# Sums of an expert's weights made by accumulating transfers, and seven products for every pair of token blocks

## The chip, the cores and the metric

The kernel runs on one core of one Trainium2 chip. The core has TensorE (matrix products into PSUM), VectorE, ScalarE and GpSimd (elementwise work), the queues that issue transfers (here those of SP and of GpSimd), and 16 DMA engines that move the data. In the profile's rows these engines are PE (with PEld for loading a matmul's stationary operand), DVE, ACT, POOL and SP. The metric is the device time of one execution in microseconds (us), lower is better. Three runs of the kernel before took 690.27, 690.28 and 691.59 us.

## The reference

Two parts follow each other. The first is attention over sorted blocks: a matrix per head is balanced by five rounds of normalisation, mixes the blocks of keys and values, and ordinary softmax attention follows. The second is a mixture of experts over the 3072 tokens that come out, and the change lies in it:

```
P = exp(logits - max); eight rounds of normalising rows and columns   # gates, tokens x 8
for e in range(8):
    h  = np.maximum(x @ w1[e], 0.0)      # x: 3072 x 512, w1[e]: 512 x 1024
    ye = h @ w2[e]                       # w2[e]: 1024 x 512
    out += P[:, e:e + 1] * ye
```

All experts process all tokens. The inputs are float32 in HBM; the products run on bfloat16 operands.

## The kernel before

Attention comes first, woven with expert 0, which is computed with plain products. Experts 1 to 7 run in the main loop. An expert's tokens are cut into three blocks of 1024 (p = 0, 1, 2), so the loop has 21 passes over (e, p); I call a pass a **pair**, numbered 0 to 20. Pair n computes the hidden layer of its own (e, p) and, at the same time, the output of the pair before it. Each pair has four steps i, which I call **slots**.

*First product, `hidden` (L475).* x and W1 are each seen as 2 x 2 blocks, and the product is made by seven block products where eight would be needed, in the manner of Strassen and Winograd: sums of W1's blocks (s1, s2, s4 in the tile `wc`, s3 over W1's own block a21) are multiplied by sums of x's blocks (`xc`, made by `sum_x` on VectorE), and the partial products are added in PSUM and on the way out. A slot makes 14 matmuls of 512 columns. VectorE's TENSOR_ADD_SAT adds two partial products and clamps below at zero in one instruction (this is the ReLU); ScalarE copies partial products p1, u2, p5 and applies the last ReLU. The four results of a slot are called c11, c12, c21, c22 and land in the tile `hT`.

*Second product.* `output` (L536) makes it with eight products: 16 matmuls of 512 columns in a slot, and two gathers (`gather`, L527: VectorE adds the gated PSUM result to the output tile `osbl`). `output7` (L561) makes it with seven: 28 matmuls of 256 columns and six gathers. It needs sums of h's blocks (`hs`, made by `sum_h` at L553: four GpSimd instructions of 128x512 a slot) and of W2's blocks (t1 to t4 in the tile `w2s` or `w2e`, made by `sum_w2`). Slots 1 to 3 use `output7` from pair 2 on; slot 0 uses `output`, since the sums of h for slot 0 would need the last result of the slot just ended. Pair 1, and the last pair's output after the loop, use `output` throughout.

*Weights' sums.* `sum_w` (L322) and `sum_w2` (L415) are generators of eight GpSimd additions or subtractions of 128x512 each. They wait in a list, and `sums` draws one of them per slot, or three at a pair's end (and in pair 1). For expert 1, `sum_w` runs during the last batch's attention. `load_w1` and `load_w2` (L82, L87) load an expert's weights from HBM and cast them to bfloat16; they are issued from GpSimd's queue. All of these are pinned, so that GpSimd takes them in the order of the program.

*Order.* The order of each engine's instructions is fixed when the kernel is built: the matmuls of `hidden` and of the output are generators that `take` (L605) draws from in turn, a few matmuls each; what is pinned keeps the program's order; the rest is placed by a scheduler. Each engine then runs its own list strictly in order and waits where an operand is not ready. Tiles come from pools with a fixed number of buffers: three for `hs`, two for `hT`, W1 and W2, so a load of expert e+1 waits for the last reader of expert e-1. Before the main loop, `balance` (L437) normalises the gates in a chain of small VectorE instructions and matmuls (L466), woven with the end of expert 0 and the hidden layer of pair 0.

Of the kernel before, what the change touches and what calls it, by code (L numbers as in the profile page):

```python
# [13 lines left out]
F32 = mybir.dt.float32  # L14
BF16 = mybir.dt.bfloat16
AF = mybir.ActivationFunctionType
# [9 lines left out]
def kernel(  # L26
# [11 lines left out]
    nc = tc.nc  # L38
# [43 lines left out]
    def load_w1(e):  # L82
        w1t[e] = wp.tile([128, 4, F], BF16, name="w1e")
        pin(nc.gpsimd.dma_start(out=w1t[e],
                                in_=moe_w1[e].rearrange("(kk k) f -> k kk f", k=128)))
# [231 lines left out]

    wct = {}  # L320

    def sum_w(e):  # L322
        wct[e] = (wcq if e % 2 == 0 else wcp).tile([128, 3, 2, F // 2], BF16, name="wc")
        for kk in range(2):
            a11, a21 = (w1t[e][:, kk, f:f + 512] for f in (0, 512))
            a12, a22 = (w1t[e][:, 2 + kk, f:f + 512] for f in (0, 512))
            s1, s2, s4 = (wct[e][:, j, kk, :] for j in range(3))
            for a, b, o, c in ((a21, a22, ALU.add, s1), (s1, a11, ALU.subtract, s2),
                               (a11, a21, ALU.subtract, a21), (a12, s2, ALU.subtract, s4)):
                pin(nc.gpsimd.tensor_tensor(out=c, in0=a, in1=b, op=o))  # L330
                yield

    with tc.tile_pool(name="ps0", bufs=8, space=bass.MemoryType.PSUM,
                      reuse_waits="tile") as ps0:
# [32 lines left out]
    with ExitStack() as c2:  # L367
        pa = c2.enter_context(tc.tile_pool(name="pa", bufs=8, space=bass.MemoryType.PSUM,
                                           reuse_waits="tile"))
        bank1 = lambda shape, dt: pa.tile(shape, dt, name="bank", tag="bank")  # L370
        ebank = lambda: bank1([128, 512], F32)
        for bb in range(1, B):
            ex = expert0(bb - 1, lambda: mps.tile([128, 8, 384], BF16, name="hTs"),
                         ebank, ebank, pin)
            at1, left = attention(bb, bank1), 16 if bb == 1 else 26
            for _ in range(28 - left):
                next(ex)
            last = 3 if bb + 1 < B else 0
            left -= last
            cut = lambda k: left * k // 12  # L380
            weave(at1, ex, 5, cut(5))
            if bb + 1 < B:
                load_batch(bb + 1, [(x, 0, 8) for x in "vkq"])
                build_r(bb + 1, nc.gpsimd, 4)
            else:
                load_w1(1)
# [23 lines left out]
    def bank():  # L410
        return bk.tile([128, 512], F32, name="bk")

    w2s = {}

    def sum_w2(e):  # L415
        w2s[e] = (wcp.tile([128, 4, 4, Dm // 2], BF16, name="w2e") if e % 2 else
                  w2q.tile([128, 4, 4, Dm // 2], BF16, name="w2s"))
        for k in (0, 2):
            b11, b12 = (w2t[e][:, k:k + 2, d:d + 256] for d in (0, 256))
            b21, b22 = (w2t[e][:, 4 + k:6 + k, d:d + 256] for d in (0, 256))  # L420
            t1, t2, t3, t4 = (w2s[e][:, j, k:k + 2, :] for j in range(4))
            for a, b, c in ((b12, b11, t1), (b22, t1, t2), (b22, b12, t3), (b21, t2, t4)):
                pin(nc.gpsimd.tensor_tensor(out=c, in0=a, in1=b, op=ALU.subtract))
                yield

# [3 lines left out]
    def sum_x(p):  # L429
        ta, tb = (slice(1024 * p + 512 * i, 1024 * p + 512 * i + 512) for i in range(2))  # L430
        b11, b12, b21, b22 = (xtT[:, k:k + 2, t] for k in (0, 2) for t in (ta, tb))
        x1, x2, x4 = (xc[:, j, :, 512 * p:512 * p + 512] for j in range(3))
        for a, b, c in ((b12, b11, x1), (b22, x1, x2), (b22, b12, b12), (b21, x2, x4)):
            pin(nc.vector.tensor_tensor(out=c, in0=a, in1=b, op=ALU.subtract))
            yield

    def balance():  # L437
# [37 lines left out]
    def hidden(e, p, i, hT):  # L475
        ta, tb = (slice(1024 * p + 512 * j, 1024 * p + 512 * j + 512) for j in range(2))
        fs = slice(128 * i, 128 * i + 128)
        xs = slice(512 * p, 512 * p + 512)

        def add(ps, wa, xa, first):  # L480
            for kk in range(2):
                nc.tensor.matmul(ps, wa[:, kk, :], xa[:, kk, :],  # L482
                                 start=(first and kk == 0), stop=(kk == 1),
                                 skip_group_check=True)
# [24 lines left out]
        u2 = wide("u2")  # L509
        nc.scalar.copy(u2, u)  # L510
        yield
        v = bank()
        add(v, s1, x1, True)
        p5 = wide("p5")
        nc.scalar.copy(p5, v)  # L515
        yield
        add(u, s3, x3, False)
        nc.vector._custom_dve(TENSOR_ADD_SAT, out=c22, in0=u, in1=p5, s0=TOP, s1=0.0)  # L518
        yield
        add(v, s4, b22, False)  # L520
        nc.vector._custom_dve(TENSOR_ADD_SAT, out=c12, in0=v, in1=u2, s0=TOP, s1=0.0)  # L521
        yield
        add(u, a22, x4, False)
        nc.scalar.activation(out=c21, in_=u, func=AF.Relu)  # L524
        yield

    def gather(e, t, c, ps):  # L527
        o = osbl[:, t, c:c + ps.shape[-1]]
        nc.vector.scalar_tensor_tensor(out=o, in0=ps, scalar=glog[:, t, e:e + 1], in1=o,  # L529
                                       op0=ALU.mult, op1=ALU.add)  # L530

    def store(e, t):
# [15 lines left out]
            yield  # L548


    hs = {}

    def sum_h(i, hT):  # L553
        s = hs[i] = hsp.tile([128, 4, 4, 128], BF16, name="hs")
        a11, a21, a12, a22 = (hT[:, f:f + 4, t + 128 * i:t + 128 * i + 128]
                              for f in (0, 4) for t in (0, 512))
        for a, b, o, c in ((a21, a22, ALU.add, 0), (s[:, 0], a11, ALU.subtract, 1),
                           (a11, a21, ALU.subtract, 2), (a12, s[:, 1], ALU.subtract, 3)):
            nc.gpsimd.tensor_tensor(out=s[:, c], in0=a, in1=b, op=o)  # L559

    def output7(e, p, i, hT):  # L561
        a, b = 8 * p + i, 8 * p + 4 + i
# [17 lines left out]
        add(x0, hT[:, 4:8, ha], b21, True)  # L580
        yield
        add(u, s2, t2, False)
        gather(e, a, 256, u)
        yield
        add(x1, s1, t1, False)
        gather(e, b, 256, x1)
        yield
        add(u, s3, t3, False)
        gather(e, b, 256, u)
        yield  # L590
        add(x1, s4, b22, False)
        gather(e, a, 0, x)
# [34 lines left out]
    take([chain, xs])  # L627
    xs = sum_x(2)
    last = (1, 0, hT)
    queue = [sum_w2(1)]  # L630

    def sums(n):
        while n and queue:
            if next(queue[0], 0) is None:
                n -= 1
            else:
                queue.pop(0)

    for n in range(1, 3 * (E - 1)):
        e, p = 1 + n // 3, n % 3  # L640
        if n == 1 or p == 0 and e + 1 < E:
            load_w1(e + 1)
            queue.append(sum_w(e + 1))
        hT = htp.tile([128, 8, 1024], BF16, name="hT")
        for i in range(4):
            if last[0] == 1:
                scale0([8 * last[1] + i, 8 * last[1] + 4 + i])
            if n > 1 and i < 3:
                sum_h(i + 1, last[2])
            next(xs, 0)  # L650
            sums(3 if n == 1 or i == 3 else 1)
            take([hidden(e, p, i, hT),
                  (output7 if n > 1 and i else output)(*last[0:2], i, last[2])])
        if n == 1 or p == 0 and e + 1 < E:
            load_w2(e + 1)
            queue.append(sum_w2(e + 1))
        last = (e, p, hT)
    for i in range(4):
        take([output(*last[0:2], i, last[2])])
# [30 lines left out]
```

## Time and profile before

| | before |
|---|---|
| median of 3 runs | 690.28 us |
| the profiled execution's own time | 690.48 us |
| its span | 688.7 us |
| TensorE busy | 666.7 us (97%) |
| VectorE busy | 474.5 us (69%) |
| GpSimd busy | 432.4 us (63%) |
| ScalarE busy | 298.0 us (43%) |
| DMA queue of GpSimd, share of 16 engines' span | 25.5% |
| DMA queue of SP | 3.4% |
| first matmul of pair 0 / pair 1 / pair 2 | 145.2 / 174.8 / 200.6 us |
| first matmul of pair 20, end of the last matmul | 645.4 / 684.1 us |

The profile is of one execution, and its span leaves out what lies around the first and last instruction; hence the two times. Busy time is an average over very different stages: attention and the start (to 145 us), the balancing chain (to 175), and the main loop, in which every pair lasts the same 24.7 us. A question about the main loop is answered by one pair. In a row of a group stand the line, the engine, the operation, what is written and read with shapes, the number of instructions, then busy time and the mean of one in ns, then the idle time of the engine just before them and what ended it. DMA-issuing instructions have rows, but are not counted as busy.

### The profile page before, as it was taken

To read this page: it belongs to the slowest core of one execution; us is meant where nothing else is said; L and a number is where in the kernel's file an instruction comes from. 1 tells how busy PE (TensorE), PEld (TensorE's weight loads), DVE (VectorE), ACT (ScalarE), POOL (GpSimd) and SP (SyncE) were. 2 spreads that over 40 slices of the span, in tenths; PEclk is the share of its full clock that TensorE was granted. 3 is DMA by queue.
4 is the path that set the end of the run, shared out by engine and by line. 5 is a ranking of instruction groups with operands and counts; after the bars stand their busy time and mean duration, and the time that the engine had idled before them with its cause. 6 is when DMAs were issued, how large, how long until landed. Compare 5 with 4: busy or idle time off the path is not lost.

```text
span 688.7 us, 12265 instructions
## 1 busy us (share of the span) xinstructions
PE 666.7 (97%) x4784; PEld 404.4 (59%) x4784; DVE 474.5 (69%) x968; ACT 298.0 (43%) x550; POOL 432.4 (63%) x411
## 2 busy tenths in 40 slices
PE   2999999999999999999999999999999999999997
PEld 1757666644446556556656655655665665565563
DVE  6627555578757778667767776767776777676773
ACT  3747646345953333343333433333333433334330
POOL 4532324202737987978977987789795998637520
PEclk9899999999999999999999999999999999999999
DMA  9897833403210340030302140034003120001213
GB/s 146 164 218 120 140 77 63 62 1 62 30 32 1 62 61 1 1 63 9 54 0 35 28 62 1 1 62 61 1 1 62 25 38 0 1 1 63 91 65 151
DMA packets 31755, 36.51 MB, mean 53 GB/s; under 512 B 2000, under 2 KB 24016, under 8 KB 31696
## 3 DMA queue, kind: packets, MB, share of 16 engines
q0 software_dynamic: 26400, 27.82, 25.5%
q1 hardware_dynamic: 5296, 7.90, 3.4%
q8 instruction: 37, 0.61, 0.4%
q14 instruction: 22, 0.18, 0.1%
HBM read 52.45 MB, written 6.29 MB: 85 GB/s over the span
## 4 chain that ended last, share of the span: by engine, by line
PE 91%; DVE 5%; ACT 1%; DMA 1%; issue 1%; SPq 0%; DVEq 0%
PE bk L482 36%; PE oacc L573 25%; PE oacc L542 13%; PE bank L297 5%; PE bank L304 5%; PE bank L232 2%; PE bank L152 1%; PE bank L243 1%; PE bank L215 1%; PE bank L196 1%; DMA vsb<-vs 1%; DVE cs L464 0%; PE bk L297 0%; PE bk L466 0%; PE bank L183 0%
## 5 line engine op out<-in xcount | busy, mean ns | idle before, releaser
L529 DVE SCALAR_TENSOR_TENSOR osbl<-oacc,glog,osbl 128x256 f32<-128x256 f32 (+1 forms) x396 | 214.8, 554 | 122.4 <-PE oacc L542 61.3
L559 POOL TENSOR_TENSOR hs<-hT 128x512 bf16<-128x512 bf16 x114 | 130.0, 1154 | 63.0 <-DVE hT L521 62.8
L482 PE MATMUL bk<-xtT,w1e 128*128 128x512 bf16 x504 | 149.9, 379 | 0.2 <-ACT u L510 0.2
L573 PEld LDWEIGHTS <-hs 128*128 128x128 bf16 x912 | 89.2, 98 | 59.0
L542 PE MATMUL oacc<-w2e,hT 128*128 128x512 bf16 x432 | 119.8, 379 | 0.0
L524 ACT ACTIVATE hT<-bk 128x512 bf16<-128x512 f32 x84 | 50.1, 597 | 153.0 <-PE bk L482 152.9
L482 PE MATMUL bk<-xc,wc 128*128 128x512 bf16 x336 | 99.9, 379 | 0.0
L573 PEld LDWEIGHTS <-hT 128*128 128x128 bf16 x684 | 66.9, 98 | 44.2
L510 ACT COPY u<-bk 128x512 f32<-128x512 f32 x84 | 49.2, 586 | 92.9 <-PE bk L482 92.8
L573 PE MATMUL oacc<-w2e,hs 128*128 128x256 bf16 x588 | 88.2, 273 | 0.0
L573 PE MATMUL oacc<-w2e,hT 128*128 128x256 bf16 x576 | 86.4, 273 | 0.0
L482 PEld LDWEIGHTS <-w1e 128*128 128x128 bf16 x672 | 65.8, 98 | 30.5 <-issue 1.4
L542 PEld LDWEIGHTS <-hT 128*128 128x128 bf16 x432 | 42.3, 98 | 50.8
L506 DVE CUSTOM_DVE_ANT_0 hT<-bk,p 128x512 bf16<-128x512 f32 x84 | 58.0, 691 | 18.4 <-PE bk L482 14.8
L559 POOL TENSOR_TENSOR hs<-hT,hs 128x512 bf16<-128x512 bf16 x57 | 65.8, 1154 | 1.5
L559 POOL TENSOR_TENSOR hs<-hs,hT 128x512 bf16<-128x512 bf16 x57 | 65.7, 1152 | 0.0
L502 ACT COPY p<-bk 128x512 f32<-128x512 f32 x84 | 49.2, 586 | 31.3 <-PE bk L482 31.3
L482 PEld LDWEIGHTS <-wc 128*128 128x128 bf16 x504 | 49.3, 98 | 22.2
L518 DVE CUSTOM_DVE_ANT_0 hT<-bk,p 128x512 bf16<-128x512 f32 x84 | 57.8, 688 | 4.5 <-PE bk L482 1.4
L515 ACT COPY p<-bk 128x512 f32<-128x512 f32 x84 | 49.3, 586 | 25.4 <-PE bk L482 25.4
L521 DVE CUSTOM_DVE_ANT_0 hT<-bk,u 128x512 bf16<-128x512 f32 x84 | 57.3, 682 | 0.1
L482 PE MATMUL bk<-xc,w1e 128*128 128x512 bf16 x168 | 50.0, 379 | 0.0
(106 smaller groups left out, 777.6 us busy)
## 6 DMA issues: line engine op xcount, KB each, us to landing
w1e<-in_moe_w_dram POOLq DMA_DIRECT2D x8, 1024.0 KB, 8.2
w2e<-in_moe_w_dram POOLq DMA_DIRECT2D x8, 1024.0 KB, 8.9
out_dram<-osbl SPq DMA_DIRECT2D x24, 256.0 KB, 2.0
vt<-in_v_dram POOLq DMA_DIRECT2D x3, 768.0 KB, 10.6
vsb<-vs SPq DMA_DIRECT2D x16, 97.5 KB, 4.6
vsb<-vs POOLq DMA_DIRECT2D x16, 97.5 KB, 4.1
qt<-in_q_dram POOLq DMA_DIRECT2D x4, 384.0 KB, 12.8
kt<-in_k_dram POOLq DMA_DIRECT2D x4, 384.0 KB, 13.4
```

The source lines that it names most:

```text
L482: nc.tensor.matmul(ps, wa[:, kk, :], xa[:, kk, :], start=(first and kk == 0), stop=(kk == 1), skip_group_check=True)
L502: nc.scalar.copy(p1, u)
L506: nc.vector._custom_dve(TENSOR_ADD_SAT, out=c11, in0=w, in1=p1, s0=TOP, s1=0.0)
L510: nc.scalar.copy(u2, u)
L515: nc.scalar.copy(p5, v)
L518: nc.vector._custom_dve(TENSOR_ADD_SAT, out=c22, in0=u, in1=p5, s0=TOP, s1=0.0)
L521: nc.vector._custom_dve(TENSOR_ADD_SAT, out=c12, in0=v, in1=u2, s0=TOP, s1=0.0)
L524: nc.scalar.activation(out=c21, in_=u, func=AF.Relu)
L529: nc.vector.scalar_tensor_tensor(out=o, in0=ps, scalar=glog[:, t, e:e + 1], in1=o, op0=ALU.mult, op1=ALU.add)
L542: nc.tensor.matmul(oacc, hT[:, fb, tt * 128:(tt + 1) * 128], w2t[e][:, fb, :], start=(fb == 0), stop=(fb == 7))
L559: nc.gpsimd.tensor_tensor(out=s[:, c], in0=a, in1=b, op=o)
L573: nc.tensor.matmul(ps, h[:, fb, :], w[:, fb, :], start=(first and fb == 0), stop=(fb == 3), skip_group_check=True)
```

## The change

1. The sums of W1's and W2's blocks are no longer made by GpSimd's arithmetic. SP copies one block into the place of the sum (SBUF to SBUF), and GpSimd issues a transfer that reads another block from HBM in float32 and adds it to what is there (`more`, `accum_op=ALU.add`). s2 starts as a copy of s1, s4 as a copy of s2, and likewise t2 of t1 and t4 of t2, so an expert has two chains of alternating copies and accumulating transfers: three copies and four transfers for W1, four copies and four transfers for W2.
2. [...] So the signs of some sums are turned: s2, t1 and others hold the negative of what they held. The sums of x are turned to match (two of four `sum_x` instructions become scalar_tensor_tensor, with a factor of -1). Where a product comes out negative, the clamp keeps the negative side (c22) and ScalarE negates it afterwards, the last ReLU takes scale=-1, and two of `output7`'s gathers use the negated gates `gneg`.
3. `output7` is used in slot 0 as well, from pair 2 to pair 20. The sums of h for slot 0 are made in two parts: three of the four blocks in slot 3 of the pair before, the last one at the start of slot 0.
4. The steps of the weights' sums and the loads have fixed slots (`plan`, `jobs`): every second slot for one expert's chain (every slot for W2 of expert 1), and within a slot behind the sums of h.

```diff
+    def more(out, src, kk, c):
+        rows, cols = out.shape[1:]
+        pin(nc.gpsimd.dma_start(
+            out=out, in_=src.rearrange("(kk k) f -> k kk f", k=128)[:, kk:kk + rows, c:c + cols],
+            accum_op=ALU.add))
 
     def sum_w(e):
+        load_w1(e)
         wct[e] = (wcq if e % 2 == 0 else wcp).tile([128, 3, 2, F // 2], BF16, name="wc")
-        for kk in range(2):
...
-                pin(nc.gpsimd.tensor_tensor(out=c, in0=a, in1=b, op=o))
-                yield
+        s1, s2, s4 = (wct[e][:, j] for j in range(3))
+        a21 = w1t[e][:, 0:2, 512:1024]
+        nc.sync.dma_start(out=s1, in_=a21)
+        yield
+        more(s1, moe_w1[e], 2, 512)
+        more(a21, moe_w1[e], 0, 0)
+        nc.sync.dma_start(out=s2, in_=s1)
+        yield
+        more(s2, moe_w1[e], 0, 0)
+        nc.sync.dma_start(out=s4, in_=s2)
+        yield
+        more(s4, moe_w1[e], 2, 0)
+        yield
+
+    def sum_w2(e):
+        if e > 1:
+            load_w2(e)
...
+        t1, t2, t3, t4 = (w2s[e][:, j] for j in range(4))
+        for t in (t1, t3):
+            nc.sync.dma_start(out=t, in_=w2t[e][:, 0:4, 256:512])
+        yield
+        more(t1, moe_w2[e], 0, 0)
+        more(t3, moe_w2[e], 4, 256)
+        nc.sync.dma_start(out=t2, in_=t1)
+        yield
+        more(t2, moe_w2[e], 4, 256)
+        nc.sync.dma_start(out=t4, in_=t2)
+        yield
+        more(t4, moe_w2[e], 4, 0)
+        yield
...
-        for a, b, c in ((b12, b11, x1), (b22, x1, x2), (b22, b12, b12), (b21, x2, x4)):
-            pin(nc.vector.tensor_tensor(out=c, in0=a, in1=b, op=ALU.subtract))
+        for a, b, c, turned in ((b11, b12, x1, False), (x1, b22, x2, True),
+                                (b22, b12, b12, False), (x2, b21, x4, True)):
+            pin(nc.vector.scalar_tensor_tensor(out=c, in0=a, scalar=-1.0, in1=b, op0=ALU.mult,
+                                               op1=ALU.subtract) if turned else
+                nc.vector.tensor_tensor(out=c, in0=a, in1=b, op=ALU.subtract))
...
-        nc.vector._custom_dve(TENSOR_ADD_SAT, out=c22, in0=u, in1=p5, s0=TOP, s1=0.0)
+        nc.vector._custom_dve(TENSOR_ADD_SAT, out=c22, in0=u, in1=p5, s0=0.0, s1=-TOP)
+        nc.scalar.activation(out=c22, in_=c22, func=AF.Copy, scale=-1.0)
...
-        nc.scalar.activation(out=c21, in_=u, func=AF.Relu)
+        nc.scalar.activation(out=c21, in_=u, func=AF.Relu, scale=-1.0)
...
-    def sum_h(i, hT):
-        s = hs[i] = hsp.tile([128, 4, 4, 128], BF16, name="hs")
...
+    def sum_h(i, hT, f0=0, f1=4):
+        if f0 == 0:
+            hs[i] = hsp.tile([128, 4, 4, 128], BF16, name="hs")
+        s1, s2, s3, s4 = (hs[i][:, j, f0:f1] for j in range(4))
...
+    nc.scalar.activation(out=gneg, in_=glog, func=AF.Copy, scale=-1.0)
+    jobs = {}
+    def plan(work, at, every):
+        for n in range(4):
+            jobs.setdefault(at + every * n, []).append(work)
+    plan(sum_w2(1), 4, 1)
     for n in range(1, 3 * (E - 1)):
         e, p = 1 + n // 3, n % 3
         if n == 1 or p == 0 and e + 1 < E:
-            load_w1(e + 1)
-            queue.append(sum_w(e + 1))
+            plan(sum_w(e + 1), 4 * n, 2)
+            plan(sum_w2(e + 1), 4 * n + 4, 2)
         hT = htp.tile([128, 8, 1024], BF16, name="hT")
         for i in range(4):
             if last[0] == 1:
                 scale0([8 * last[1] + i, 8 * last[1] + 4 + i])
+            if n > 1 and i == 0:
+                sum_h(0, last[2], 3)
             if n > 1 and i < 3:
                 sum_h(i + 1, last[2])
+            if i == 3 and n + 1 < 3 * (E - 1):
+                sum_h(0, hT, 0, 3)
             next(xs, 0)
-            sums(3 if n == 1 or i == 3 else 1)
+            for work in jobs.get(4 * n + i, ()):
+                next(work)
             take([hidden(e, p, i, hT),
-                  (output7 if n > 1 and i else output)(*last[0:2], i, last[2])])
-        if n == 1 or p == 0 and e + 1 < E:
-            load_w2(e + 1)
-            queue.append(sum_w2(e + 1))
+                  (output7 if n > 1 else output)(*last[0:2], i, last[2])])
```

More of the change, by code (lines that the diff above doesn't have):

```diff
@@ L316, in expert0 @@
             yield from expert(0, bb * S + c * 384, 384, hsb, hbank, obank, keep, hold)
-    wct = {}
+    wct, w2s = {}, {}
+    def more(out, src, kk, c):
[3 more added lines that the diff above has]
+            accum_op=ALU.add))
     def sum_w(e):
+        load_w1(e)
         wct[e] = (wcq if e % 2 == 0 else wcp).tile([128, 3, 2, F // 2], BF16, name="wc")
-        for kk in range(2):
[L325 to L329, printed above, removed]
-                pin(nc.gpsimd.tensor_tensor(out=c, in0=a, in1=b, op=o))
-                yield
+        s1, s2, s4 = (wct[e][:, j] for j in range(3))
[14 more added lines that the diff above has]
+            load_w2(e)
+        w2s[e] = (wcp.tile([128, 4, 4, Dm // 2], BF16, name="w2e") if e % 2 else
+                  w2q.tile([128, 4, 4, Dm // 2], BF16, name="w2s"))
+        t1, t2, t3, t4 = (w2s[e][:, j] for j in range(4))
[11 more added lines that the diff above has]
+        yield
     with tc.tile_pool(name="ps0", bufs=8, space=bass.MemoryType.PSUM,
@@ L385 @@
             else:
-                load_w1(1)
                 sums = sum_w(1)
@@ L411, in bank @@
         return bk.tile([128, 512], F32, name="bk")
[L413 to L424, printed above, removed]
     xc = xcp.tile([128, 3, 2, N // 2], BF16)
@@ L523, in hidden, with gather @@
         add(u, a22, x4, False)
-        nc.scalar.activation(out=c21, in_=u, func=AF.Relu)
+        nc.scalar.activation(out=c21, in_=u, func=AF.Relu, scale=-1.0)
         yield
-    def gather(e, t, c, ps):
+    def gather(e, t, c, ps, sign=1):
         o = osbl[:, t, c:c + ps.shape[-1]]
-        nc.vector.scalar_tensor_tensor(out=o, in0=ps, scalar=glog[:, t, e:e + 1], in1=o,
+        g = glog if sign > 0 else gneg
+        nc.vector.scalar_tensor_tensor(out=o, in0=ps, scalar=g[:, t, e:e + 1], in1=o,
                                        op0=ALU.mult, op1=ALU.add)
@@ L548, in output @@
             yield
+    gneg = mpc.tile([128, NT, E], F32)
     hs = {}
-    def sum_h(i, hT):
-        s = hs[i] = hsp.tile([128, 4, 4, 128], BF16, name="hs")
-        a11, a21, a12, a22 = (hT[:, f:f + 4, t + 128 * i:t + 128 * i + 128]
+    def sum_h(i, hT, f0=0, f1=4):
+        if f0 == 0:
+            hs[i] = hsp.tile([128, 4, 4, 128], BF16, name="hs")
+        s1, s2, s3, s4 = (hs[i][:, j, f0:f1] for j in range(4))
+        a11, a21, a12, a22 = (hT[:, f + f0:f + f1, t + 128 * i:t + 128 * i + 128]
                               for f in (0, 4) for t in (0, 512))
-        for a, b, o, c in ((a21, a22, ALU.add, 0), (s[:, 0], a11, ALU.subtract, 1),
-                           (a11, a21, ALU.subtract, 2), (a12, s[:, 1], ALU.subtract, 3)):
-            nc.gpsimd.tensor_tensor(out=s[:, c], in0=a, in1=b, op=o)
+        for a, b, o, c in ((a21, a22, ALU.subtract, s1), (s1, a11, ALU.subtract, s2),
+                           (a11, a21, ALU.subtract, s3), (a12, s2, ALU.add, s4)):
+            nc.gpsimd.tensor_tensor(out=c, in0=a, in1=b, op=o)
     def output7(e, p, i, hT):
@@ L582, in output7 @@
         add(u, s2, t2, False)
-        gather(e, a, 256, u)
+        gather(e, a, 256, u, -1)
         yield
@@ L588, in output7 @@
         add(u, s3, t3, False)
-        gather(e, b, 256, u)
+        gather(e, b, 256, u, -1)
         yield
@@ L629 @@
     last = (1, 0, hT)
[L630 to L637, printed above, removed]
+    nc.scalar.activation(out=gneg, in_=glog, func=AF.Copy, scale=-1.0)
[4 more added lines that the diff above has]
+    plan(sum_w2(1), 4, 1)
     for n in range(1, 3 * (E - 1)):
```

## The prediction

> **What bounds the kernel now.** I read the busy shares first, then the stretches of one pair of token blocks, the list of waits, GpSimd's groups and timeline, and the landing times of transfers. From the page:
>
> ```profile
> PE 666.7 (97%) x4784; PEld 404.4 (59%) x4784; DVE 474.5 (69%) x968; ACT 298.0 (43%) x550; POOL 432.4 (63%) x411
> ```
>
> TensorE is the bound. The stretches of one pair, cut at the first matmul of each slot (a slot is one step i of the inner loop); columns: window, its length, then busy time (instructions) of each engine, granted clock, DMA share, GB/s:
>
> ```profile
> 398.27:404.75 6.48, 6.48 (x32) 2.94 (x30) 3.54 (x6) 2.72 (x5) 6.46 (x7) 1.00 0.92 126
> 404.75:410.83 6.08, 6.08 (x44) 4.09 (x42) 4.76 (x9) 2.00 (x4) 6.08 (x6) 1.00 0.25 42
> 410.83:416.91 6.08, 6.08 (x45) 4.12 (x43) 4.87 (x10) 2.36 (x5) 6.00 (x7) 1.00 0.00 0
> 416.91:422.99 6.08, 6.08 (x45) 4.12 (x43) 4.87 (x10) 2.36 (x5) 2.28 (x3) 1.00 0.00 0
> ```
>
> A slot with eight products in the second layer (the first row) lasts 6.48 us, one with seven 6.08, and TensorE fills both. The same pattern runs from pair 2 to pair 20. The waits from 200 to 665 us name no TensorE line; GpSimd's are:
>
> ```profile
> POOL hs L559 <- DVE hT L521: 62.8, 9, 15.0
> POOL w1e L84 <- PE bk L482: 25.5, 5, 6.9
> POOL w2e L89 <- PE oacc L573: 11.3, 5, 3.1
> ```
>
> GpSimd has slack, but it runs in order, and TensorE reads its sums. Its groups, and the transfers:
>
> ```profile
> L559 POOL TENSOR_TENSOR hs<-hT 128x512 bf16<-128x512 bf16 x114 | 130.0, 1154 | 63.0 <-DVE hT L521 62.8
> L89 POOL DMA_DIRECT2D w2e<-in_moe_w_dram x8 | 7.4, 928 | 11.3 <-PE oacc L573 11.3
> L84 POOL DMA_DIRECT2D w1e<-in_moe_w_dram x8 | 6.4, 794 | 62.6 <-PE bk L297 36.7 <-PE bk L482 25.5 <-issue 0.3
> ```
> ```profile
> w1e<-in_moe_w_dram POOLq DMA_DIRECT2D x8, 1024.0 KB, 8.2
> w2e<-in_moe_w_dram POOLq DMA_DIRECT2D x8, 1024.0 KB, 8.9
> out_dram<-osbl SPq DMA_DIRECT2D x24, 256.0 KB, 2.0
> ```
> And where GpSimd meets a pair's end (slot start at 422.99):
> ```profile
> 416.75 2.40 POOL L423 TENSOR_TENSOR w2e<-w2e 128x512 bf16<-128x512 bf16 x2
> 422.87 2.27 POOL L559 TENSOR_TENSOR hs<-hT 128x512 bf16<-128x512 bf16 x2 [3.73 <-DVE hT L521]
> ```
>
> Two such instructions in a row end 2.27 apart and not 2.31: one costs 1.115 us of GpSimd's time. T below is the start of a pair's slot 0.
>
> **Seven products in slot 0.** From pair 2 to pair 20, 19 slots change from 16 matmuls of 512 columns to 28 of 256: 19 x (6.475 - 6.08) = -7.5 us. VectorE's gathers go from 2 x 0.745 to 5 x 0.480 + 0.745 in that slot, which makes it one of the 4.87 us slots above; three of these in a row already run at 6.08. TensorE's order in the loop is the old pattern, repeated. This is the gain; the rest is whether something makes TensorE wait.
>
> **Signs.** (1) ScalarE negates c22, 84 x 0.59 (the row of its 128x512 copies): 50 us on an engine with 2.36 of 6.08 us used. In the slot it sits between the copy to p5 and the last Relu. VectorE ends c22 4.9 us into a slot, so the negation ends near 5.5, ahead of c12 at 5.95, which the sums need anyway: 0. If ScalarE were full, up to 0.59 a slot. (2) Two of the four sums per token block become scalar_tensor_tensor of 128x1024. The tensor_tensor beside no GpSimd work took 0.68; by the slope between the gathers (0.480 at 256 columns, 0.745 at 512) the new form takes up to 1.27, so 0 to +0.6 each. Two lie in the balancing chain after 145 us, where TensorE idled 2.25 us over 140 to 175 waiting for column sums. TensorE's new order puts about 0.4 us more matmuls into some of those intervals. I take +0.3, ends -0.5 and +1.2. (3) The negated gates: one 0.45 us activation after that chain, first used in pair 2. (4) Other constants: 0.
>
> **Weights' sums leave GpSimd.** 16 instructions an expert go, 7 x 16 x 1.115 = 125 us, off the path: GpSimd waits 63 us for hT. In return come, per expert, eight accumulating transfers that GpSimd issues and seven copies that SP issues; each of GpSimd's waits for a copy, each copy for a transfer before it. SP has nothing else to do before the stores of the last expert. Issue: 0.54 (96 packets) to 0.93 (1024 packets) by the rows; I take 0.65 for W1's (256) and 0.8 for W2's (512).
>
> A 1 KB packet of a plain casting load, which reads 2 KB of float32, holds its DMA engine 0.098 us (packets of the trace, as the others here); one of 1040 bytes copied out of SBUF 0.047 undisturbed, 0.133 under other traffic. No accumulating transfer is in this trace. A packet of one reads both its source and its destination: 0.098 + 0.047 = 0.145 as estimate, so 16 packets on each engine take 2.35 us. The lower end is the plain load's 1.6 us; the upper is 4.7, three times that, as the 1040-byte packets rose to three times theirs when they met other reads. I take 2.35, since packets in this trace follow the bytes that they read.
>
> **Hidden sums for slot 0.** Eight more GpSimd instructions per pair: four of 384 columns in slot 3, four of 128 in the next slot 0. By 1.115 for 512 and about 0.2 fixed (its 128x128 rows take 0.2 to 0.3): 0.85 and 0.36, so 4.85 per pair, 92 us in all. The budget per pair of 24.3 us: 1.4 + 12 x 1.115 + 3.4 = 18.2 us, and transfers' issue, at most five, 3.8. It fits if GpSimd does not stand still.
>
> **Where it stands still.** In six pairs (2, 4, 7, 10, 13, 16) GpSimd's order is: rest of sum 0 and sum 1, transfer s2, load W2, sums 2 and 3, transfer s4, transfers t1 and t3, then sum 0 of the next pair. Sum 0 starts at T-0.1 (above), so s2 is issued at T+5.8 and the load of W2 at T+6.5. Its packets stand behind s2's: those begin 0.7 after the issue's end, T+7.15, and end at 9.5; W2's take 7.05 (125.61 to 132.66 for the load issued at 123.97), so 16.55, plus 0.65 for the copy of s2 to s4 in between and 0.2 to land: T+17.4. SP then copies t1 and t3, 0.6 apart, 32 packets of 512 bytes per engine each. A 256 KB store lands in 2.0 with 0.66 us of packets (8 of 2 KB at 0.083); with 0.87 (0.027 each, on the line through the 1040-byte and 2 KB packets), and s4's transfer beside them, I get T+20.5 and T+21.6. GpSimd was free for t1 at T+17.0, so it stands 3.5 us; t3 is issued by T+22.4. Then sum 0 for the next pair, 3.4 + 1.1 until its s2 is complete: T+26.9. TensorE needs it in the third group of the next slot 0: groups of the two layers alternate, 0.434 us each, so that group starts 2.17 into the slot and takes its last operand at 2.5, T+26.8. Stall 0.2 us x 6 = +1.2. If transfers cost as plain loads: T+21.5, no stall, 0.7 spare; at three times, T+24.8, 2.5 x 6 = +15.
>
> In other pairs the margin is wider. Where W1 is loaded: issue T+5.8, landing +8.2, copy +2.4 = T+16.5, when GpSimd has just finished sum 3 at T+15.6. The old code blocked GpSimd on the release of W1 and W2 (25.5 and 11.3 us of waits); both loads now stand behind sum 1, when their buffers are long free.
>
> **The start.** For expert 1, load W1 is still issued at 106.7 and lands at 114.9. Then three times a copy (2.4) and a transfer (1.5 to start, 2.35, 0.2): 134 for s4's landing; the old sums ended near 124. Its first use is some 7 us after 145.2, so 0; at 10 us a transfer it would begin to cost. GpSimd's other work of that stretch (queries' copies) precedes it; W2's load behind it moves from 124 to about 132, and is needed after 174. For W2 of expert 1 the last transfer, t4, now stands behind slot 3's sum 0, issue near 198, landing 202 to 203; needed at 206: 0, with 3 us to spare.
>
> **Sum.** 690.48 (profiled execution: span 688.7 and 1.8 around it; it is 0.2 over the median) - 7.5 + 1.2 + 0.3 = 684.5.
>
> **Rivals.** (a) Slower: accumulating transfers, or their issue, are dearer than that. Place: the six pair ends above. The sum turns where each stall passes 1.2 us, t3 issued past T+23.4: packets of 0.21 us (2.1 times plain), or 0.3 us more for each issue. At three times 690.5 - 7.5 + 15 + 0.3 = 698, at four times 708. For it: s2's transfer stands in W2's ring, and nothing here shows its rate. Against: packets follow bytes read. (b) No stall at all, 683.3, if they cost as plain loads. (c) The second read costs a whole packet like the first: 2 x 0.098, 3.1 us, t3 issued at T+23.2, a stall of 1.0, 689.3. For it: no packet here reads two places, so the sum of two rows is untried; against: the destination's bytes are half the source's.
>
> [...]
>
> (d) VectorE holds slot 0 at 6.48, as four dense slots now follow each other: 690.5, no change. Against: 4 x 4.87 is 19.5 of 24.3. (e) The balancing chain or the start waits 2 to 4 us more: 686 to 688; for it, that chain alone made TensorE wait before.
>
> **How the numbers follow.** The runs spread 1.3 us, 0.2%, about what can be told from no change (688.9 to 691.7). The forecast with (b): 0.40, 682.5 to 685.5. Larger stalls under 1 us, or (e), up to 688.9: 0.15. Within 0.2%, (c) and (d): 0.09. Slower, by (a): 0.36; of this some 0.15 lies over 706, and below 681.5 I leave 0.03. Range 681.5 to 706; the forecast's own is 682.5 to 685.5.
>
> **What would show it.** All slots of pairs 2 to 20 at 6.08; GpSimd's waits naming t1's and t3's copies, 3 to 4 us, six times; TensorE's gathered-sum line with at most 0.3 us of waits for GpSimd at pairs' ends. The forecast is wrong if W2's load lands past T+19, if accumulating packets hold an engine 0.2 us, or if the first slots of expert 1 wait for its weights.

## The result, and the profile after

The kernel after takes 729.65 us (median of four runs, 727.57 to 731.35), the kernel before 690.27 in runs on the same chip: a ratio of 1.057, 95% interval 1.054 to 1.060. It is 39 us slower. I had put 684.5 us as the likeliest and 706 as the upper end. The prediction is wrong.

The profiled execution of after took 731.35 us, its span is 729.4 us: 40.7 us more than the span of before (688.7). The busy shares of its page:

```profile
PE 676.3 (93%) x5012; PEld 430.6 (59%) x5012; DVE 505.4 (69%) x1044; ACT 349.7 (48%) x635; POOL 472.1 (65%) x507
```

TensorE is busy for 93% of the span instead of 97%, and no other engine came near its limit: VectorE and ScalarE have the busy time that the change gives them, GpSimd stands at 65%. So TensorE waits, but not for an engine that is full. I cut the main loop into slots as before (a slot begins with the first matmul of its 14 in `hidden`). Nearly every slot from pair 2 to pair 20 lasts 6.08 us, the first slots included. Seven first slots do not:

| slot 0 of pair | 3 | 4 | 5 | 8 | 11 | 14 | 17 |
|---|---|---|---|---|---|---|---|
| length, us | 13.16 | 7.15 | 14.55 | 15.01 | 12.36 | 14.12 | 14.62 |
| TensorE idle in it | 4.22 | 0.90 | 5.76 | 6.19 | 4.53 | 5.07 | 5.46 |
| half clock begins, lasts | 230.2, 6.8 | none | 288.2, 6.8 | 370.2, 6.8 | 452.1, 3.4 | 530.6, 6.8 | 612.5, 6.8 |

Over 6.08 us each, these are 48.4 us: 32.1 of idle time and 16.3 that the idle time leaves unexplained. The account of the span: +48.4, -7.5 for the first slots that went from 6.475 to 6.08, +0.3 because pair 2 starts at 200.87 instead of 200.59, and -0.5 after the last matmul, in sum +40.7.

Six of the seven are the pair ends after pairs 2, 4, 7, 10, 13 and 16, the places that rival (a) named. I show the one between pairs 16 and 17. The stretches of pair 16's slot 0 and of pair 17's first two slots (window, its length, busy time of PE, PEld, DVE, ACT and POOL with instructions, granted clock, DMA share, GB/s):

```profile
581.13:587.21 6.08, 6.08 (x44) 4.11 (x42) 4.88 (x10) 2.99 (x6) 6.08 (x9) 1.00 0.01 5
605.45:620.06 14.61, 9.15 (x44) 4.99 (x42) 5.61 (x10) 2.98 (x6) 13.71 (x16) 0.77 0.46 62
620.06:626.14 6.08, 6.08 (x45) 4.11 (x42) 4.50 (x9) 2.98 (x6) 6.00 (x6) 1.00 0.60 86
```

The first row is what I expected of every slot 0. In the second TensorE has the same 44 matmul rows, 5.5 us in which it does nothing, and a mean clock of 0.77. Its timeline there (start, length of the row, line, operation, and in brackets the idle time before it and what ended that):

```profile
607.18 0.59 PE L507 MATMUL bk<-xc,wc 128*128 128x512 bf16 x2
611.61 0.50 PE L604 MATMUL oacc<-w2s,hs 128*128 128x256 bf16 x3 [3.83 <-POOL hs L590]
613.74 0.40 PE L604 MATMUL oacc<-w2s,hs 128*128 128x256 bf16 x1 [1.63 <-POOL hs L590]
614.78 1.06 PE L604 MATMUL oacc<-w2s,hs 128*128 128x256 bf16 x4
```

TensorE waits twice for the sum s2 of the hidden layer (`hs`): first for the part of three blocks, then for the last block. And then the same two matmuls of 512 columns that took 0.59 us before the wait take 1.06: the granted clock is half until 619.3. Who is late is told by the waits between 200 and 700 us (engine, line, what is waited for: total, times, longest):

```profile
POOL hs L590 <- DVE hT L547: 33.7, 18, 3.1
PE oacc L604 <- POOL hs L590: 32.1, 13, 4.9
POOL w2e L326 <- DMA w2e<-w2e: 14.7, 4, 5.3
POOL w2s L326 <- DMA w2s<-w2e: 12.7, 3, 5.6
```

TensorE's 32.1 us are all for GpSimd's sums. The last two rows are GpSimd's waits in front of the accumulating transfers to t1 and t3 (L326) for SP's copies: seven waits at the six pair ends, 27.4 us. I had expected 3 to 4 us, six times. GpSimd's timeline at the same pair end (pair 16 starts at T = 581.13):

```profile
587.06 1.17 POOL L326 DMA_DIRECT2D wc<-in_moe_w_dram  x1
587.81 1.37 POOL L89 DMA_DIRECT2D w2e<-in_moe_w_dram  x1
...
599.77 1.21 POOL L326 DMA_DIRECT2D wc<-in_moe_w_dram  x1 [1.66 <-DMA wc<-wc]
606.27 2.62 POOL L326 DMA_DIRECT2D w2e<-in_moe_w_dram  x2 [5.29 <-DMA w2e<-w2e]
607.83 2.86 POOL L590 TENSOR_TENSOR hs<-hT 128x384 bf16<-128x384 bf16 x2
...
613.26 0.42 POOL L590 TENSOR_TENSOR hs<-hs,hT 128x128 bf16<-128x128 bf16 x1
```

and SP's, which issues the two copies that the 5.29 us are for:

```profile
600.61 1.32 SPq L356 DMA_DIRECT2D w2e<-w2e  x2
```

Read from the top: s2's transfer, the load of W2 behind it, six sums of h, then 1.66 us of waiting for the copy of s2 to s4, the transfer for s4, 5.29 us of waiting for the copies t1 and t3, the two transfers, and only then sum 0 for the next pair, which TensorE has needed since T+26.8 = 607.9. The transfers (median us from issue to landing) say why SP could not begin earlier:

```profile
w1e<-in_moe_w_dram POOLq DMA_DIRECT2D x8, 1024.0 KB, 8.2
w2e<-in_moe_w_dram POOLq DMA_DIRECT2D x8, 1024.0 KB, 12.2
...
w2s<-w2e SPq DMA_DIRECT2D x6, 256.0 KB, 5.2
```

W1 lands after 8.2 us as before; W2, behind s2's transfer, after 12.2 instead of 8.9. The copies of t1 and t3 take 5.2 us.

### The profile page after: what moved, and what is told of

Its sections match the earlier page's. It is cut to its first block, busy times and chain, and to the rows that moved or that the text cites. A ratio compares the mean times of both kernels' runs of the same rounds, so it can differ in the third digit from the quotient of the medians.

```text
span 729.4 us, 13204 instructions
## 1 busy us (share of the span) xinstructions
PE 676.3 (93%) x5012; PEld 430.6 (59%) x5012; DVE 505.4 (69%) x1044; ACT 349.7 (48%) x635; POOL 472.1 (65%) x507
## 4 chain that ended last, share of the span: by engine, by line
PE 78%; POOL 7%; DMA 6%; DVE 4%; issue 2%; ACT 2%; POOLq 0%; DVEq 0%; SPq 0%; ACTq 0%
PE bk L507 30%; PE oacc L604 28%; POOL hs L590 5%; PE bank L297 5%; PE bank L304 4%; PE oacc L569 3%; DMA w2s<-w2e 2%; PE bank L232 2%; DMA w2e<-in_moe_w_dram 2%; DMA w2e<-w2e 1%; PE bank L152 1%; POOL w2e L326 1%; PE bank L215 1%; PE bank L243 1%; PE bank L196 1%
## 5 line engine op out<-in xcount | busy, mean ns | idle before, releaser
L590 POOL TENSOR_TENSOR hs<-hT 128x512 bf16<-128x512 bf16 (+2 forms) x190 | 200.2, 1145 | 40.4 <-DVE hT L547 39.5
L556 DVE SCALAR_TENSOR_TENSOR osbl<-oacc,glog,osbl 128x512 f32<-128x512 f32 (+1 forms) x320 | 171.9, 556 | 66.7 <-PE oacc L604 51.4
L604 PEld LDWEIGHTS <-hs 128*128 128x128 bf16 x1216 | 121.8, 101 | 121.6 <-POOL hs L590 37.8
L604 PE MATMUL oacc<-w2e,hs 128*128 128x256 bf16 x784 | 122.9, 280 | 15.5 <-POOL hs L590 15.5
L556 DVE SCALAR_TENSOR_TENSOR osbl<-oacc,gneg,osbl 128x256 f32<-128x256 f32 x152 | 72.9, 480 | 75.1 <-PE oacc L604 74.8
L604 PE MATMUL oacc<-w2e,hT 128*128 128x256 bf16 x768 | 115.2, 273 | 0.0
L590 POOL TENSOR_TENSOR hs<-hs,hT 128x512 bf16<-128x512 bf16 (+2 forms) x95 | 107.5, 1132 | 0.1
L590 POOL TENSOR_TENSOR hs<-hT,hs 128x512 bf16<-128x512 bf16 (+2 forms) x95 | 96.5, 1016 | 2.7
L544 ACT ACTIVATE hT<-hT 128x512 bf16<-128x512 bf16 x84 | 53.0, 630 | 87.1 <-DVE hT L543 87.0
L604 PE MATMUL oacc<-w2s,hs 128*128 128x256 bf16 x432 | 68.6, 282 | 16.7 <-POOL hs L590 16.7
L507 PEld LDWEIGHTS <-wc 128*128 128x128 bf16 x504 | 50.2, 100 | 12.1 <-issue 2.0
## 6 DMA issues: line engine op xcount, KB each, us to landing
w2e<-in_moe_w_dram POOLq DMA_DIRECT2D x8, 1024.0 KB, 12.2
```

Source lines behind the costliest of these rows:

```text
L507: nc.tensor.matmul(ps, wa[:, kk, :], xa[:, kk, :], start=(first and kk == 0), stop=(kk == 1), skip_group_check=True)
L544: nc.scalar.activation(out=c22, in_=c22, func=AF.Copy, scale=-1.0)
L556: nc.vector.scalar_tensor_tensor(out=o, in0=ps, scalar=g[:, t, e:e + 1], in1=o, op0=ALU.mult, op1=ALU.add)
L604: nc.tensor.matmul(ps, h[:, fb, :], w[:, fb, :], start=(first and fb == 0), stop=(fb == 3), skip_group_check=True)
```

## The experiments

My theory after this reading: the transfers cost about what I had said, and it is their order that is wrong. GpSimd stands in front of t1's and t3's transfers until two queues have drained, and the sums that TensorE needs stand behind it. The rivals were that accumulating transfers as such are too dear, that some other part of the change (signs, VectorE, the start) costs time, and that seven products in slot 0 cannot be fed by GpSimd at all.

### Only the steps of the chains moved

The same transfers, copies, signs and products. For experts 3 to 7 the load of W2 stays where it was and W2's transfers come two to four slots later (t1 and t3 four, t2 six and t4 ten slots behind the load), so that GpSimd finds the copies landed; expert 2's whole chain starts in pair 1, two slots earlier (`m` is the first slot of an expert's chain):

```diff
-    def plan(work, at, every):
-        for n in range(4):
-            jobs.setdefault(at + every * n, []).append(work)
+    def plan(work, *slots):
+        for n in slots:
+            jobs.setdefault(n, []).append(work)
...
-            plan(sum_w(e + 1), 4 * n, 2)
-            plan(sum_w2(e + 1), 4 * n + 4, 2)
+            m = 4 * n
+            plan(sum_w(e + 1), m, m + 2, m + 4, m + 6)
+            if n == 1:
+                plan(sum_w2(e + 1), m + 2, m + 5, m + 7, m + 9)
+            else:
+                plan(sum_w2(e + 1), m + 4, m + 8, m + 10, m + 14)
```

> The changed kernel, with the steps of W2's chain moved: for experts 3 to 7 the load stays where it was, the transfers t1 and t3 come two slots later (slot 0 of the next pair), t2 four slots and t4 eight slots after the load; for expert 2 the chain starts in pair 1. Theory: all that is lost is GpSimd standing still for the copies of t1 and t3 at the end of six pairs, so that sum 0 of the next pair is late, and TensorE's clock after such an idle stretch. Then all slots from pair 2 to pair 20 last 6.08, TensorE has no wait for GpSimd over 0.5 us there, and the time is 690.3 - 7.5 + 0.3 = 683 (682 to 686). Rival: GpSimd has simply too much to do with the accumulating transfers (issue of 1.2 us each, slower instructions beside them); then the stalls move to other pairs and the time stays over 700.

Measured: 682.92 us (682.32 to 683.0, four runs), ratio to before 0.989 (0.9875 to 0.9904). It beats both kernels, by 7.5 and 46.7 us. All slots of pairs 2 to 20 last 6.08 us, TensorE has no wait for GpSimd there, and the clock is full from 40 to 681 us. Its page, its transfers, and GpSimd at the end of pair 16:

```profile
PE 659.6 (97%) x5012; PEld 426.4 (63%) x5012; DVE 503.7 (74%) x1044; ACT 349.9 (51%) x635; POOL 472.4 (69%) x507
```
```profile
w2e<-in_moe_w_dram POOLq DMA_DIRECT2D x8, 1024.0 KB, 12.2
```
```profile
560.46 1.21 POOL L326 DMA_DIRECT2D wc<-in_moe_w_dram  x1 [2.19 <-DVE osbl L556]
561.24 2.24 POOL L590 TENSOR_TENSOR hs<-hT 128x384 bf16<-128x384 bf16 x2
...
571.54 2.56 POOL L326 DMA_DIRECT2D w2e<-in_moe_w_dram  x2
```

The load of W2 still takes 12.2 us, and at this pair end the two copies still take 4.3 and 5.8 from issue to landing. They cost nothing, because GpSimd goes on from s4's transfer to sum 0 at once and issues t1 and t3 eleven microseconds later. With another order the whole loss is gone, then; and what is left is the gain that the prediction gave to seven products, 19 x (6.475 - 6.08) = 7.5 us.

### One transfer out of the copies' way

W1's last transfer, s4, goes two slots later, so that it does not lie between the load of W2 and the copies of t1 and t3. All else as in after.

```diff
-            plan(sum_w(e + 1), 4 * n, 2)
-            plan(sum_w2(e + 1), 4 * n + 4, 2)
+            m = 4 * n
+            plan(sum_w(e + 1), m, m + 2, m + 4, m + 8)
+            plan(sum_w2(e + 1), m + 4, m + 6, m + 8, m + 10)
```

> The changed kernel, with one transfer moved: s4 of W1 is issued two slots later (slot 0 of the next pair, behind the sums of h), and so no longer just ahead of the copies of t1 and t3. In the changed kernel those copies land 5.5 us after they are issued, and their packets start only when s4's are through. Theory: s4's packets hold them up. Then they land about 3.3 us after issue, each of the six stalls is some 2 us shorter, and the time falls by 12 to 20 us, to 709 to 717 (the shorter stall may or may not cost TensorE's clock as well). Rival: such copies take 5.5 us in any case, or GpSimd is held by something else: then the time stays within 2 us of 729.7.

Measured: 714.34 us (712.47 and 716.21), ratio 1.035 (1.031 to 1.038): 15 us less than after, as expected. The copies land after 2.8 us, and the slots 0 of pairs 5, 8, 11, 14 and 17 last 8.6 to 10.7 us instead of 12.4 to 15.0. Transfers and waits (the second from TensorE's waits between 200 and 700 us):

```profile
w2s<-w2e SPq DMA_DIRECT2D x6, 256.0 KB, 2.8
```
```profile
PE oacc L604 <- POOL hs L590: 13.5, 11, 1.6
PE bk L507 <- DMA wc<-in_moe_w_dram: 7.8, 1, 7.8
```

So s4's packets in front of the copies cost 2.4 us of landing time, and with what follows from it 23 of the 40 us that those five slots lose in after (over 6.08 us they lose 17 here). The second wait is a side effect of my edit: expert 2's s4 comes too late for its first use, and slot 0 of pair 3 lasts 17.07 us, 7.8 us of them this wait.

### W2's steps ahead of W1's in each slot

One swap of two lines: GpSimd issues the load of W2 before s2's transfer, and t1's and t3's before s4's.

```diff
+            plan(sum_w2(e + 1), 4 * n + 4, 2)
             plan(sum_w(e + 1), 4 * n, 2)
-            plan(sum_w2(e + 1), 4 * n + 4, 2)
```

> The changed kernel with the two plans swapped, so that in each slot W2's step goes ahead of W1's: the load of W2 ahead of transfer s2, the copies and transfers t1 and t3 ahead of s4's, on GpSimd's queue as on SP's. No step changes its slot. Theory: what was late is the load of W2 behind s2 (landing 12.2 us after issue instead of 8.9) and then the copies behind s4; now the load lands near T+15.5, the copies near T+18.5, and with the issue of three transfers GpSimd starts sum 0 near T+22, about 1 us too late for TensorE: six stalls of 0.5 to 1.5 us without slow clock, 686 to 694. Rival: GpSimd's issue of the transfers and its slower instructions beside them make the delay, so that the order does not matter: above 715.

Measured: 693.47 us (median of ten, 691.96 to 698.94), ratio 1.005 (1.003 to 1.007). Two lines exchanged win back 36 of the 39 us.

```profile
w2e<-in_moe_w_dram POOLq DMA_DIRECT2D x8, 1024.0 KB, 9.7
...
w2s<-w2e SPq DMA_DIRECT2D x6, 256.0 KB, 2.9
```
```profile
PE oacc L604 <- POOL hs L590: 6.9, 8, 1.6
```

The load of W2 lands 2.5 us earlier, the copies 2.3, and the slots 0 that were 12.4 to 15 us are 6.6 to 7.4 (pair 4's is 10.49, with a short stretch of half clock). Over 6.08 us these seven slots still lose 10.3 us, which eats the gain of 7.5. Six of them have stalls of 0.3 to 1.1 us; the prediction had 0.2 for after, and 1.0 in its rival (c).

### The sums made by arithmetic again

Transfers undone: GpSimd adds the blocks, the weights are loaded as before; seven products in slot 0, the signs and the hidden sums of after stay. With the turned signs all of them are additions here too; their number and shapes are those of before.

```diff
...
+            for a, b, c in ((a21, a22, s1), (s1, a11, s2), (a11, a21, a21), (a12, s2, s4)):
+                pin(nc.gpsimd.tensor_tensor(out=c, in0=a, in1=b, op=ALU.add))
+                yield
...
```

> The changed kernel with the weights' sums made by GpSimd's additions again (all of them additions, as the turned signs allow), drawn and loaded as in the kernel before; seven products in slot 0 and the turned signs stay. It tells whether the transfers were needed. GpSimd's work for three pairs: 3 x 18.2 of sums of h, 16 x 1.115 of weights, 1.7 for two loads, 74.1 us, against 73.0 of TensorE. So GpSimd is about 1 us short per expert and TensorE waits at least that: 683 + 7 x 1 = 690, between 685 and 700, since each wait of several us may cost TensorE's clock too. Rival: the order on GpSimd's queue (loads that wait for TensorE ahead of the rest of sum 0) makes every pair's slot 0 wait: over 705.

Measured: 709.66 us (709.45 to 712.46), ratio 1.029 (1.026 to 1.032). I had about 690 as the likeliest and 700 as the end; it is worse, where the rival of that expectation had put it (over 705). The page, TensorE's wait, and the stretch of pairs 3 to 5 (columns as above):

```profile
PE 663.3 (94%) x5012; PEld 425.2 (60%) x5012; DVE 505.9 (71%) x1044; ACT 350.3 (49%) x635; POOL 527.5 (75%) x563
```
```profile
PE oacc L581 <- POOL hs L567: 19.3, 12, 3.2
```
```profile
226.84:304.48 77.64, 73.46 (x506) 49.04 (x504) 58.36 (x109) 35.82 (x61) 77.05 (x81) 1.00 0.17 28
```

Here no queue is in the way (W2 lands after 8.8 us). GpSimd has 16 additions per expert and eight more instructions per pair, and the first slots of pairs 3 to 13 and of pair 16 each wait 0.9 to 3.2 us for its sums; those of pairs 14, 15 and from 17 on, the pair that makes the last of the weights' sums, last 6.08. In pairs 3 to 5 GpSimd is at work for 77.05 of 77.64 us (and for as much of pairs 6 to 8 and 9 to 11), where four slots of 6.08 a pair would be 73.0. So an engine that is busy 75% over the whole execution is full in the stretch that counts: it is its work, and not only the order on its queue. The rival "GpSimd cannot feed seven products" holds for this form; with the transfers seven products in slot 0 pay.

### Slot 0 with eight products again

The transfers, copies and signs of after, but `output` in slot 0 and no hidden sums for it.

```diff
-            if n > 1 and i == 0:
-                sum_h(0, last[2], 3)
...
-            if i == 3 and n + 1 < 3 * (E - 1):
-                sum_h(0, hT, 0, 3)
...
-                  (output7 if n > 1 else output)(*last[0:2], i, last[2])])
+                  (output7 if n > 1 and i else output)(*last[0:2], i, last[2])])
```

> The changed kernel with eight products in slot 0 again, and without the sums of h for slot 0; transfers, signs and slots of the steps as changed. Theory: GpSimd is as late as before, but its next result is needed only 6.48 + 2.2 us into the pair, and it has it near 5.5; so nothing waits, slot 0 lasts 6.48, the others 6.08, and the time is that of the kernel before plus 0 to 1: 690 to 691.5. Rival: the transfers and copies themselves, or the negation on ScalarE and the turned sums, slow the slots or the start: over 693.

Measured: 690.62 us (ten runs), ratio 1.0002 (0.9992 to 1.0012). With the transfers as late as in after (W2 12.1 us, copies 5.3), nothing is lost when TensorE does not need GpSimd at the start of a pair. So signs, negations, gates, the start and the transfers' traffic together cost nothing that can be measured (there is one wait of 2.0 us, in pair 5), and the loss of after needs both parts: the late transfers, and an early reader of what stands behind them. The first experiment, which differs from this one in the products of slot 0 and also in the places of the steps, is 690.6 - 682.9 = 7.7 us faster, about the 7.5 of the slots' lengths.

### Plain loads in the place of accumulating ones

The transfers keep their sizes, places and waits, but write over the copies instead of adding to them, so the weights' sums are left out of the computation.

```diff
-            out=out, in_=src.rearrange("(kk k) f -> k kk f", k=128)[:, kk:kk + rows, c:c + cols],
-            accum_op=ALU.add))
+            out=out, in_=src.rearrange("(kk k) f -> k kk f", k=128)[:, kk:kk + rows, c:c + cols]))
```

> The changed kernel with all accumulating transfers turned into plain casting loads of the same bytes to the same places (so the weights' sums are left out; what is computed is another thing, the instructions and waits stay). Packets should hold an engine 98 ns where they held 140 (1 KB), and some 56 where they held 84 (512 bytes). Theory: the stalls come from the order of transfers and copies, and accumulating as such has only 0.7 us of s2 and 0.7 of s4 in each: the six stalls shrink by 1.5 us or a little more, the time to 712 to 722. Rival: accumulating is the cause; then the stalls vanish and the time is below 700.

Measured: 707.72 us (706.14 and 709.3), ratio 1.024 (1.021 to 1.028): between the two expectations. The same pair end as above (T is 561.50 here):

```profile
567.42 0.74 POOL L326 DMA_DIRECT2D wc<-in_moe_w_dram  x1
568.16 0.91 POOL L89 DMA_DIRECT2D w2e<-in_moe_w_dram  x1
...
579.63 0.74 POOL L326 DMA_DIRECT2D wc<-in_moe_w_dram  x1 [1.60 <-DMA wc<-wc]
584.83 1.55 POOL L326 DMA_DIRECT2D w2e<-in_moe_w_dram  x2 [4.46 <-DMA w2e<-w2e]
586.39 1.80 POOL L589 TENSOR_TENSOR hs<-hT 128x384 bf16<-128x384 bf16 x2
```

The pattern is the same, and mostly shorter at two steps. Both copies have landed at T+23.6 instead of T+25.4, since s4's packets, in front of them, are through at T+21.6 instead of T+23.4; so sum 0 begins at T+24.9 instead of T+26.7. And its first two instructions take 1.76 us (to the next start at 588.15) instead of 2.07. The row of an issue is 0.74 instead of 1.17 to 1.21, but GpSimd's next instruction begins 0.7 to 0.8 us after the start of a transfer's issue in both kernels. The stalls shrink from 4.2 to 6.2 us to 2.0 to 4.5, and half clock appears three times, each time 3.4 us, instead of six times. So the adding has 22 us in this order; the other 25, from 682.9 with a good order to 707.7, are lost by plain transfers too.

### Idle time and the clock

The 16.3 us that idle time leaves unexplained stand beside intervals of half clock. To test whether idle time alone brings them, I took the kernel of the first experiment, which has neither, and repeated the first instruction of sum 1 in eight pairs, 5 to 14 times, so that TensorE waits in slot 1 with no unusual transfer near.

```diff
-            nc.gpsimd.tensor_tensor(out=c, in0=a, in1=b, op=o)
+            for _ in range(1 + again):
+                nc.gpsimd.tensor_tensor(out=c, in0=a, in1=b, op=o)
+            again = 0
...
+    repeats = {4: 5, 7: 6, 10: 7, 13: 8, 16: 9, 18: 10, 19: 12, 20: 14}
```

> The kernel with the later steps, in which TensorE runs without a wait, and in eight pairs the first instruction of sum 1 repeated 5 to 14 times on GpSimd (pairs 4, 7, 10, 13, 16, 18, 19, 20: 5, 6, 7, 8, 9, 10, 12, 14 times, 1.115 us each), so that TensorE waits in slot 1 for a known time. GpSimd has about 4.2 us to spare there, so TensorE should stand 1.4, 2.5, 3.6, 4.7, 5.8, 7.0, 9.2 and 11.4 us. Theory: an idle stretch of TensorE over about 3 us is followed by up to 6.8 us at half clock, so the slots after the longer waits grow by their wait and up to 3.4 us more, those after the first two by their wait alone; in sum 46 us of waits and 10 to 20 us of slow clock: 739 to 750. Rival: the half clock in the changed kernel has nothing to do with the waits before it; then each slot grows by its wait alone and the time is near 729.

Measured: 804.68 us (one run). The waits came out much longer than I had set them, 7.0 to 18.3 us, since other instructions of GpSimd came in between; the short ones that would have shown how long a wait must be were not had. Half clock followed in all eight, and nowhere else in the main loop. Pair 7's slot 1, with one wait of 7.72 us (stretch, then TensorE's rows):

```profile
338.02:353.88 15.86, 8.14 (x44) 4.77 (x42) 5.08 (x10) 2.98 (x6) 15.78 (x15) 0.78 0.12 11
```
```profile
339.75 0.59 PE L507 MATMUL bk<-xc,wc 128*128 128x512 bf16 x2
348.07 1.03 PE L606 MATMUL oacc<-w2e,hs 128*128 128x256 bf16 x4 [7.72 <-POOL hs L591]
348.89 1.06 PE L507 MATMUL bk<-xc,wc 128*128 128x512 bf16 x2
...
352.14 0.59 PE L507 MATMUL bk<-xtT,wc 128*128 128x512 bf16 x2
```

The clock fell at 345.1, while TensorE still waited, and came back at 352.0. The slot is 15.86 - 6.08 - 7.72 = 2.1 us longer than its wait explains; over the eight it is 1.8 to 2.8 us. So in this kernel the clock halved with no unusual transfer near, after idle time alone, and each of the eight waits cost itself and those 1.8 to 2.8 us more.

## Why the prediction was wrong

**Seven products in slot 0**: right. -7.5 predicted; the slots are 6.08 us, and the kernel with moved steps is 7.5 us faster than before. VectorE, rival (d), held nothing.

**Signs and the start**: not contradicted. Pair 2 starts 0.3 us later, as predicted, but that agreement is luck: in the profiled executions of the nine kernels it starts anywhere from 200.3 to 202.4 us, at 200.9 and at 202.2 in kernels that are alike up to there. The kernel with eight products shows nothing measurable (1.0002). The first slots of expert 1 wait for no weights.

**Weights' sums leave GpSimd**: the packet's price was right. An accumulating packet of 1 KB in SBUF (2 KB read from HBM) holds its DMA engine for 0.140 us in the median, against the estimate 0.145 and 0.098 for a plain load. Rival (c), two full reads at 0.196, is not what happened: an adding packet is 1.43 times as long as a plain one, with a destination of half the source's bytes. That it reads its destination as well was my estimate's premise; the traces show its time alone. The price of the issue held as well: the rows are 1.2 us long instead of 0.65 to 0.8, but GpSimd's next instruction starts 0.75 to 0.79 us after an accumulating issue's start (587.06 to 587.81, 606.27 to 607.06 to 607.83). So rival (a) had the place of the loss, but neither of its causes, packets or issues dearer than I had them.

**Where it stands still**: this is the step that failed. The place and the order of the waits are as written there; the sizes of the chain's terms are not, and one overlap, of the copies with s4's transfer, did not take place. At the end of pair 16:

| | predicted | measured | late by |
|---|---|---|---|
| load of W2 issued | T+6.5 | T+6.7 | 0.2 |
| it has landed, SP may copy | T+17.4 | T+19.4 | 2.0 |
| both copies have landed | T+21.6 | T+25.4 | 3.8 |
| sum 0 of the next pair starts | T+22.4 | T+26.7 | 4.3 |
| its s2 is complete | T+26.9 | T+32.6 | 5.7 |
| TensorE needs it | T+26.8 | T+26.8 | |

Four terms were too small, and they add up, as they lie on one chain:

1. *The load of W2, +2.0.* Its packets began when s2's were through, as I had it, but that was near T+10.4 and not T+9.5, and they took 8.7 us, not 7.05 and 0.65.
2. *The copies, +1.8.* I had them run beside s4's transfer. They waited for it: SP issued them at 600.61 and 601.28, the transfer's packets ran from 601.69 to 604.38, and the copies' first packet is at 604.04, 3.4 us after the issue; in the second experiment, with no transfer in the way, it comes after 1.3 us. The copy of s2 to s4 was late too: issued at 591.92, its first packets came at 596.2, in the middle of W2's. That is where GpSimd's 1.66 us are from. The second experiment shows this term by itself, 5.2 us against 2.8.
3. *From landing to issue, +0.5.* I had t3 issued as soon as its copy has landed, and one issue of 0.8 us from there to sum 0. It took 1.3: t1's copy landed at 605.73, GpSimd's issue began 0.54 us later at 606.27, t3's behind it at 607.06, and sum 0 at 607.83. With plain transfers it is the same 0.54 from landing to issue.
4. *Sum 0 itself, +1.4.* 5.9 us until the last block's s2 instead of 4.5. The instructions right behind the two accumulating issues are slow here: the third of 384 columns starts 2.07 us after the first, where it is 1.76 with plain transfers, and the next 1.73 us later, where it is 0.98.

The chain of estimates ended 0.1 us after the time when TensorE needs the sum, so that every error in it went straight into the stall, and the errors all had one sign. The rival's turning point was a stall of 1.2 us; the stalls are 4.2 to 6.2.

**What was not in the prediction at all** is the clock. Six stalls of 4.2 to 6.2 us brought six stretches of half clock, 16.1 us in sum (1.8 to 3.1 each beyond the wait; the other 0.2 are pair 4's). With stalls of 0.2 us, as predicted, I would expect none: pair 4's slot 0, with 0.90 us idle, had none. Rival (a) gave 708 for packets four times as dear as plain ones; that sum, too, took the stall for the whole of the loss. (The chances of the prediction add up to 1.03.)

The seventh slow slot, pair 4's 1.07 us, lies one pair on, where W1 and W2 of experts 2 and 3 follow each other closely; that this is its cause was not tested.

## What to carry to other kernels

When work moves from arithmetic to transfers, the question is not what the transfers cost but what stands behind each wait on the queue that issues them: here a swap of two lines was worth 36 us, and moving the waiting steps a few slots later turned 39 us lost into 7.5 us won. A margin of a tenth of a microsecond over a chain of four estimates is no margin, so look for the order that makes the estimates not matter. And where TensorE may stand for 4 us or more, as in after and in the last experiment, I would price the stall at itself plus 2 to 3 us, for the clock: six stalls of 4.2 to 6.2 us and eight of 7.0 to 18.3 us cost 1.8 to 3.1 us each on top.

## What the runs showed of the hardware

*The clock after idle time.* In the trace of after, and in that of before, every change of the granted clock lies on one grid of steps of 3.413 us (in after, from 230.2 to 288.2 are 17 of them, from 288.2 to 370.2 are 24). Counted by these steps, from pair 2 to the last matmul, the full clock of after stayed full after every step in which TensorE was idle for at most 1.31 us, and was half after all six steps with 2.69 to 3.41 us, with no step in between; from half, it was full again after the six steps with at most 0.53 us, and stayed half after the five with 1.24 to 1.82 us. So a step did not have to be idle throughout: 2.69 of its 3.41 us were enough here. With plain loads two waits of 0.55 and 1.64 us, at 227.4 and 228.5, were followed by matmuls of 512 columns at 1.06 us for two instead of 0.59, from 231.2 on; with the sums made by arithmetic one wait of 3.19 us was followed by the same, from 492.9 on.

*SP's packets beside GpSimd's.* At the end of pair 16 the copies issued by SP gave way to s4's transfer of 256 KB, issued by GpSimd. In after not one of the copies' packets began before 604.04, while s4's ran at up to 34 in a quarter of a microsecond; from 604.25 to 605.5 the copies moved 143 to 174 in each quarter. In the kernel of the first experiment, at the same place, the copies moved 121 packets in a quarter of a microsecond before s4's packets came, 2 to 15 while those ran at 28 to 34, and 150 after them. With plain transfers it was the same: copies issued at 580.74, and SP's packets begin at 582.8, when the last of GpSimd's are at hand. Beside the 1 MB load of W2 it was so in part: the copy of s2 to s4 got its first packet 4.2 us after its issue, but from then on both ran together (from 597.0 to 597.75, 19 to 20 packets of 2 KB in a quarter of a microsecond beside 24 to 28 of W2's). I had taken such transfers to run side by side. Why they did so in one place and not in the other is not shown by these runs.

*GpSimd after issuing.* An accumulating issue had a row of 1.2 us against 0.74 for the same transfer without adding, though the next instruction started as soon (0.75 and 0.74 us later); and at the end of pair 16 the sums behind two of them were 1.1 us late in all (steps of 2.07 and 1.73 us instead of 1.76 and 0.98). Why is not shown by these runs.
